# k^T v over all 128 partitions: five of nine tokens on the lower half, four on the upper, two heads at a time

## The chip, the cores and the metric

The kernel runs on one core of a Trainium2 chip. The metric is the device time of one execution in microseconds (us). Every kernel was run several times, and beside each experiment the kernel before ran on the same chip. A run more than 1.5% above the fastest of its kernel is called slow. TensorE is PE in the profile (PEld is its weight loading), VectorE is DVE, ScalarE ACT, GpSimd POOL, SyncE SP.

## The reference, cut to what matters

```python
batch, n_heads, seq, head_dim = (8, 8, 576, 64)          # q, k, v in float32
kv  = einsum('bhsd,bhse->bhde', k, v)                    # k^T v, 64 x 64 per head
out = einsum('bhsd,bhde->bhse', q, kv)
out = out / rms(out) * g_norm
x   = out.transpose(0, 2, 1, 3).reshape(4608, 512)
# then a mixture of 8 experts: x + gate * expert(x) where x @ w_skip > 0, else x
```

Attention reads q, k and v of eight batches, 1152 KB each. k^T v sums over the 576 tokens of a head.

Of the kernel before, what the change touches and what calls it, by code (L numbers as in the profile page):

```python
# [8 lines left out]
FP32 = mybir.dt.float32  # L9
# [8 lines left out]
def kernel(  # L18
# [9 lines left out]
    moe_w2: bass.AP,  # L28
    out: bass.AP,
):  # L30



# [29 lines left out]
    nc = tc.nc  # L63
    B, H, S, D = q.shape
    DM = H * D
    N = B * S
    P = 128
    C = S // 64
    CT = 4
# [25 lines left out]
    kv_pool = attn.enter_context(tc.tile_pool(name="kv", bufs=3))  # L95
    q_pool = attn.enter_context(tc.tile_pool(name="q", bufs=3))
    setup = attn.enter_context(tc.tile_pool(name="setup", bufs=1))
# [3 lines left out]
    xb_pool = attn.enter_context(tc.tile_pool(name="xb", bufs=2))  # L101
    ps_kv = attn.enter_context(tc.tile_pool(name="ps_kv", bufs=1, space=bass.MemoryType.PSUM))
# [7 lines left out]
    kts, vts, qts = {}, {}, {}  # L110

    def load(pool, tag, src, b):
        t = pool.tile([P, 4, C, D], FP32, tag=tag, name=tag)
        nc.sync.dma_start(out=t[:, :, :, :].rearrange("p j c d -> p j (c d)"),
                          in_=src[b].rearrange("(j a) (p c) d -> (a p) j (c d)", a=2, c=C))
        return t

    def load_first(b):

        for name, pool, src, to in (("k", kv_pool, k, kts), ("v", kv_pool, v, vts)):  # L120
            to[b] = pool.tile([P, 4, C, D], FP32, tag=name, name=name)
        for js in (slice(0, 2), slice(2, 4)):
            for src, t in ((k, kts[b]), (v, vts[b])):
                nc.sync.dma_start(
                    out=t[:, js, :, :].rearrange("p j c d -> p j (c d)"),
                    in_=src[b].rearrange("(j a) (p c) d -> (a p) j (c d)", a=2, c=C)[:, js, :])

    def load_kv(b):
        if b < B:
            kts[b] = load(kv_pool, "k", k, b)  # L130
            vts[b] = load(kv_pool, "v", v, b)

    def load_q(b):
        if b < B:
            qts[b] = load(q_pool, "q", q, b)
# [3 lines left out]



    load_first(0)
    load_q(0)

    room = xb_pool.tile([P, NQ, 2, DM], FP32, tag="xb", name="xb")
# [57 lines left out]
    for a in range(2):  # L203
        r = slice(a * 64, (a + 1) * 64)
# [4 lines left out]
    for w in range(2):  # L209
        nc.vector.tensor_copy(out=swap[:, w * 64:(w + 1) * 64],  # L210
                              in_=ident[:, (1 - w) * 64:(2 - w) * 64])
# [52 lines left out]
    for lo, m in kinds:  # L264

        t = keep.tile([P, P], FP32, name=f"again{lo}_{m}")
# [38 lines left out]


    kvns, kvTs, kvss = {}, {}, {}

    sum_ps = ps_kv.tile([P, 2, 512], FP32, name="sum_ps")[:, :, 0:2 * D].rearrange("p a (u d) -> p a u d", u=2)
    sw_ps = g_ps[:, 0:2 * PK]  # L310
    kvT_ps = g_ps[:, 0:2 * P].rearrange("p (u x) -> p u x", u=2)
    lg_ps = g_ps[:, 2 * PK:2 * PK + 8 * G].rearrange("p (u a w g) -> p u a w g", u=2, a=2, w=2)
# [4 lines left out]
        assert ap[-1] == [1, PK]  # L317
        return bass.AP(x.tensor, x.offset, ap[:-1] + [[PK - G, 2], [1, G]])

    def state(b, third):  # L320

        kt, vt = kts[b], vts[b]
        for i in range(6 * third, 6 * third + 6):
            u, c = divmod(i, C)
            for w in range(2):
                for a in range(2):
                    r = slice(a * 64, (a + 1) * 64)
                    nc.tensor.matmul(  # L328
                        out=sum_ps[w * 64:(w + 1) * 64, a, u, :],
                        lhsT=kt[r, 2 * u + w, c, :], rhs=vt[r, 2 * u + w, c, :],  # L330
                        start=(c == 0), stop=(c == C - 1), skip_group_check=True)
        if third < 2:
            return
        kvn = kvn_pool.tile([P, 2, PK], FP32, tag="kvn", name="kvn")
        nc.scalar.copy(out=kvn[:, :, G:G + 2 * D].rearrange("p u (a d) -> p a u d", a=2), in_=sum_ps)
        kvns[b] = kvn
# [44 lines left out]
    def turn(n):  # L381
        _, b, i, u = units[n]
        if i is None:
            qTs[n] = q8s[b][:, u, :, :, :]
            return
        ps = ps_q.tile([P, 2, 2, 2, 64], FP32, tag="q", name="q_ps")
        for w in range(2):
            for hf in range(2):
                c = 4 * i + 2 * hf
                nc.tensor.transpose(out=ps[:, w, :, hf, :], in_=qts[b][:, 2 * u + w, c:c + 2, :],  # L390
                                    identity=ident[:, :])
        qT = att_pool.tile([P, 2, 2, P], FP32, tag="qT", name="qT")
        nc.scalar.copy(out=qT[:, :, :, :].rearrange("p w a t -> p (w a t)"),
                       in_=ps[:, :, :, :, :].rearrange("p w a h t -> p (w a h t)"))
        qTs[n] = qT
# [282 lines left out]
    def slot_rows(cols, pool, tag):  # L678

        n = cols.stop - cols.start  # L680
        rows = pool.tile([P, n], I32, tag=f"rows{tag}", name="rows")
        nc.vector.tensor_single_scalar(out=rows[:, :], in_=srow[:, cols], scalar=float(N),
                                       op=ALU.add)
        src = pool.tile([P, n], I32, tag=f"src{tag}", name="src")
        nc.vector.scalar_tensor_tensor(out=src[:, :], in0=rows[:, :], scalar=N, in1=rows[:, :],
                                       op0=ALU.is_lt, op1=ALU.mult)
        return rows, src
# [7 lines left out]
    def early():  # L695
# [10 lines left out]
        def put():  # L706
# [14 lines left out]
            in_offset=bass.IndirectOffsetOnAxis(ap=src[:, 0:1], axis=0))  # L721

    load_kv(1)
    load_kv(2)
    load_q(1)


    zero = setup.tile([64, DM], FP32)
    nc.gpsimd.memset(zero[:, :], 0.0)
    for b in range(KNOWN // S // 4 * 4, KNOWN // S):  # L730
        nc.gpsimd.dma_start(
            out=out[b * S:(b + 1) * S, :].rearrange("(p c) d -> p c d", c=C)[:, C - 1, :],
            in_=zero[:, :])

    todo = {}

    def at(step, part, job):
        todo.setdefault((step, part), []).append(job)
# [6 lines left out]
    for n, (_, b, i, _) in enumerate(units):  # L745
        if i is not None:
            starts.setdefault(b, n)
    parts = [lambda b: state(b, 0), lambda b: state(b, 1), lambda b: state(b, 2), state_t, state_m, state_s]
    for part in parts[:5]:
        part(0)  # L750
    turn(0)
    for part in parts[5:]:
        part(0)
    for b, n in starts.items():
        if b:
            for i, part in enumerate(parts):
                at(max(n - 6 + i, (0, 0, 1, 1, 2, 3)[i]), "pe", lambda b=b, part=part: part(b))
        def loads(b=b):
            load_kv(b + 3)
            load_q(b + 2)  # L760
        at(n, "end", loads)
# [47 lines left out]
    with tc.tile_pool(name="wpool_b", bufs=1, reuse_waits="tile") as wpool_b, \  # L809
# [456 lines left out]
        rows, src = slot_rows(slice(0, NCOL), slot_pool, "")  # L1266
# [28 lines left out]
        with tc.For_i(1, n_rounds, 1):  # L1295
# [8 lines left out]
                out=left[:, :].rearrange("p (r c) -> p r c", c=CK),  # L1304
# [3 lines left out]
            rows, src = slot_rows(slice(0, NCOL), slot_pool, "")  # L1308
# [35 lines left out]
```

## The kernel before: what the change touches

A load of k puts the heads with j of 0 to 3 in the tile, a = 0 on partitions 0 to 63 and a = 1 on partitions 64 to 127. A partition holds nine consecutive tokens of one head: 9 x 64 x 4 = 2304 bytes in one packet. One DMA fills all 128 partitions.

```python
def load(pool, tag, src, b):
    t = pool.tile([P, 4, C, D], FP32, tag=tag, name=tag)          # P = 128, C = 9, D = 64
    nc.sync.dma_start(out=t[:, :, :, :].rearrange("p j c d -> p j (c d)"),
                      in_=src[b].rearrange("(j a) (p c) d -> (a p) j (c d)", a=2, c=C))
    return t
```

The products of one batch are issued in three parts. By the slices of the program, four 64x64 products go together: two halves of the input partitions (a) by two halves of the output partitions (w).

```python
def state(b, third):
    kt, vt = kts[b], vts[b]
    for i in range(6 * third, 6 * third + 6):
        u, c = divmod(i, C)
        for w in range(2):
            for a in range(2):
                r = slice(a * 64, (a + 1) * 64)
                nc.tensor.matmul(out=sum_ps[w * 64:(w + 1) * 64, a, u, :],
                                 lhsT=kt[r, 2 * u + w, c, :], rhs=vt[r, 2 * u + w, c, :],
                                 start=(c == 0), stop=(c == C - 1), skip_group_check=True)
    ...
```

Output rows are stored in two halves, partitions 0 to 63 from GpSimd's queue and 64 to 127 from SyncE's. SyncE's queue is in order (in the profile before, two stores stand in it from 64.84 us for 10.22 us, and k is issued only at 75.15), so this store also stands ahead of later loads:

```python
    nc.gpsimd.dma_start(out=rows[0], in_=xb[0:64, ...])
    return lambda: nc.sync.dma_start(out=rows[1], in_=xb[64:128, ...])     # issued one step later
    ...
    def loads(b=b):                    # at the end of the first step of batch b
        load_kv(b + 3)
        load_q(b + 2)
```

## Time and profile before

| | before |
|---|---|
| time, median of 4 runs beside the changed kernel | 418.05 us (416.71 to 419.89) |
| span of the profiled run, granted PE clock | 418.8 us, 0.935 |
| products of k^T v on PE | 26.3 us busy |

Four lines of the page: the busy time of the engines, the granted PE clock in forty slices of 10.5 us (tenths of full speed), and two of the DMA queues (packets, MB, share of 16 engines).

```profile
PE 368.3 (88%) x4292; PEld 316.6 (76%) x4292; DVE 250.8 (60%) x621; ACT 139.1 (33%) x368; POOL 118.8 (28%) x185
...
PEclk9975999889966599999999999999999999999995
...
q1 hardware_dynamic: 26688, 66.59, 45.3%
...
q8 instruction: 36, 0.59, 0.6%
```

PE is the busiest engine over the whole, but up to 73 us the DMA engines are hardly ever free. q1 is SyncE's queue, with all loads in it. q8, of the kind that the page calls instruction, moves 36 packets of about 16 KB (0.59 MB).

### The profile page before, as it was taken

What the parts mean: (1) busy time and instruction counts of PE and PEld (TensorE: products, weight loads), DVE (VectorE), ACT (ScalarE), POOL (GpSimd) and SP (SyncE); (2) the same over time, 40 slices, a digit from 0 to 9 for tenths busy, and PEclk for the clock granted to TensorE, in tenths of its full rate; (3) what the DMA queues carried; (4) which work ended last, traced back from release to release, by engine and by line L of the source; (5) the groups of instructions that cost most, each with busy time, mean ns of one, the idle gap of its engine ahead of it and who ended that gap; (6) DMA issues with size and microseconds to landing.
All of it is one profiled execution on the core that took longest, in us unless ns stands there. A gap on an engine that the chain in (4) does not pass through costs nothing. (4 is left out here: it accounts for less than half of the span.)

```text
span 418.8 us, 10468 instructions
## 1 busy us (share of the span) xinstructions
PE 368.3 (88%) x4292; PEld 316.6 (76%) x4292; DVE 250.8 (60%) x621; ACT 139.1 (33%) x368; POOL 118.8 (28%) x185
## 2 busy tenths in 40 slices
PE   3879999688684599999999999999999999999970
PEld 3768888576563486958977987988988988989950
DVE  2132576638898763166565775766776866778520
ACT  1253676446553131212420440430440431423300
POOL 3012667535546614012203301121212203201010
PEclk9975999889966599999999999999999999999995
DMA  8999999894128995055351651752772663501010
GB/s 292 392 390 391 318 396 394 223 383 122 42 71 317 354 347 176 5 223 184 120 202 48 233 210 51 250 201 69 242 225 83 230 229 102 203 1 52 0 42 8
DMA packets 31339, 81.89 MB, mean 196 GB/s; under 512 B 1866, under 2 KB 1874, under 8 KB 31284
## 3 DMA queue, kind: packets, MB, share of 16 engines
q1 hardware_dynamic: 26688, 66.59, 45.3%
q0 software_dynamic: 4576, 14.54, 10.4%
q8 instruction: 36, 0.59, 0.6%
q14 instruction: 19, 0.16, 0.1%
q10 hardware_dynamic: 20, 0.02, 0.0%
HBM read 66.80 MB, written 14.61 MB: 194 GB/s over the span
## 5 line engine op out<-in xcount | busy, mean ns | idle before, releaser
L1013 PE MATMUL bank<-xt,w 128*128 128x144 f32 (+3 forms) x336 | 56.4, 291 | 0.0
L1023 ACT COPY p<-bank 128x144 f32<-128x144 f32 (+4 forms) x70 | 21.0, 300 | 105.6 <-PE bank L1013 103.9
L1013 PEld LDWEIGHTS bank<-xt,w 128*128 128x128 f32 x336 | 47.8, 190 | 1.9 <-DVE bank L1017 1.4
L1017 DVE TENSOR_TENSOR bank<-bank,p 128x144 f32<-128x144 f32 (+4 forms) x70 | 23.8, 341 | 40.2 <-PE bank L1013 38.7
L430 PE MATMUL o_ps<-kvn,qT 64*64 64x73 f32 (+1 forms) x384 | 35.6, 276 | 8.6 <-DVE xl L459 5.7
L430 PEld LDWEIGHTS o_ps<-kvn,qT 64*64 64x64 f32 (+1 forms) x384 | 30.1, 178 | 15.8 <-issue 8.2
L1155 POOL DMA_INDIRECT out_dram<-xg,rows x16 | 16.2, 1014 | 79.1 <-DVE xg L1152 78.5
L492 POOL TENSOR_TENSOR xb<-xl,g_b 128x512 f32<-128x512 f32 x32 | 38.0, 1188 | 0.0
L1013 PE MATMUL bank<-xs,s 128*128 128x144 f32 (+3 forms) x224 | 37.3, 292 | 0.0
L945 PE MATMUL bank<-w,ht 128*32 128x128 f32 (+2 forms) x448 | 36.1, 321 | 0.0
L430 PE MATMUL o_ps<-kvs,qT 64*64 64x73 f32 (+1 forms) x384 | 34.9, 277 | 0.9 <-issue 0.9
L442 DVE TENSOR_REDUCE rs<-sq 128x8 f32<-128x512 f32 x36 | 24.5, 680 | 15.0 <-ACT sq L434 14.5
L1013 PEld LDWEIGHTS bank<-xs,s 128*128 128x128 f32 x224 | 31.6, 190 | 1.0 <-ACT p L1023 0.3
L905 POOL DMA_INDIRECT xg<-out_dram,src x15 | 15.7, 1047 | 56.5 <-PE bank L1013 36.2
L328 PE MATMUL sum_ps<-v,k 64*64 64x64 f32 x1152 | 26.3, 245 | 6.1 <-issue 5.3
L945 PEld LDWEIGHTS bank<-w,ht 128*32 128x32 f32 (+2 forms) x448 | 20.6, 121 | 14.6 <-issue 11.8
L1155 POOL DMA_INDIRECT out_dram<-xg,arows x8 | 9.0, 1130 | 77.0 <-DVE xg L1152 76.7
L459 DVE TENSOR_TENSOR xl<-o_ps,rs 128x584 f32<-128x584 f32 x36 | 27.6, 767 | 4.8 <-DVE rs L456 0.5
L328 PEld LDWEIGHTS sum_ps<-v,k 64*64 64x64 f32 x1152 | 22.9, 156 | 10.0 <-issue 9.3
L430 PEld LDWEIGHTS o_ps<-kvs,qT 64*64 64x64 f32 (+1 forms) x384 | 29.4, 178 | 1.2 <-issue 1.0
L476 POOL TENSOR_TENSOR lp<-xl 128x36 f32<-128x36 f32 x36 | 9.2, 255 | 66.5 <-DVE xl L459 66.3
L434 ACT ACTIVATE sq<-o_ps 128x512 f32<-128x512 f32 x36 | 21.5, 597 | 19.4 <-PE o_ps L430 19.2
(190 smaller groups left out, 744.8 us busy)
## 6 DMA issues: line engine op xcount, KB each, us to landing
w<-in_moe_w_dram SPq DMA_DIRECT2D x16, 2048.0 KB, 10.4
q<-in_q_dram SPq DMA_DIRECT2D x8, 1152.0 KB, 14.9
k<-in_k_dram SPq DMA_DIRECT2D x7, 1152.0 KB, 12.4
v<-in_v_dram SPq DMA_DIRECT2D x7, 1152.0 KB, 15.1
out_dram<-xb SPq DMA_DIRECT2D x8, 512.0 KB, 17.0
out_dram<-xb POOLq DMA_DIRECT2D x8, 512.0 KB, 7.6
k<-in_k_dram SPq DMA_DIRECT2D x2, 576.0 KB, 5.3
v<-in_v_dram SPq DMA_DIRECT2D x2, 576.0 KB, 8.4
```

Of the source, the lines that this page charges most:

```text
L328: nc.tensor.matmul(out=sum_ps[w * 64:(w + 1) * 64, a, u, :], lhsT=kt[r, 2 * u + w, c, :], rhs=vt[r, 2 * u + w, c, :], start=(c == 0), stop ...
L430: nc.tensor.matmul(out=ps[to, r, cols], lhsT=lhsT, rhs=kv[rows, u, a * KD:(a + 1) * KD], start=True, stop=True, skip_group_check=True)
L434: nc.scalar.activation(out=sq[:, :, :, :], in_=heads(ps, G, G + 2 * D), func=ACT.Square)
L442: nc.vector.tensor_reduce(out=rs[:, :, :], in_=sq[:, :, :, :].rearrange("p r w (a d) -> p r (w a) d", a=2), axis=AX.X, op=ALU.add)
L459: nc.vector.tensor_tensor(out=xl[:, :, :, :].rearrange("p r w (a k) -> p r (w a) k", a=2), in0=ps[:, :, 0:2 * PK].rearrange("p r (h k) -> ...
L492: nc.gpsimd.tensor_tensor(out=xb[:, :, 4 * u * D:(4 * u + 4) * D].rearrange("p r (w x) -> p r w x", w=2), in0=xl[:, :, :, G:G + 2 * D], in ...
L905: nc.gpsimd.indirect_dma_start(out=x_of(xg, off, m), out_offset=None, in_=cut_rows(m)[:, :], in_offset=bass.IndirectOffsetOnAxis(ap=idx[:, ...
L945: nc.tensor.matmul(out=yps[q * m:(q + 1) * m, 0:n], lhsT=ht[:, f, off:off + m], rhs=w_sb[r][1][:, f, q * n:(q + 1) * n], start=(f == 0), s ...
L1013: nc.tensor.matmul(out=out, lhsT=lhsT(i), rhs=rhs(i), start=start and i == 0, stop=i == k - 1, skip_group_check=True)
L1017: nc.vector.tensor_tensor(out=to, in0=x, in1=y, op=ALU.add)
L1023: nc.scalar.copy(out=t, in_=x)
L1155: ins = nc.gpsimd.indirect_dma_start(out=cut_rows(m)[:, :], out_offset=bass.IndirectOffsetOnAxis(ap=rows[:, col:col + 1], axis=0), in_=x, ...
```

## The change

The intent is to sum over all 128 input partitions at once. If both halves of them hold tokens of the same head, one 128x64 product replaces two 64x64 ones, and two heads share the 128 output partitions. Nine tokens don't split evenly, so a lower partition takes five and the upper partition beside it in the sum takes four; the fifth is multiplied over 64 rows alone. This makes 40 matmuls a batch. One DMA now fills 64 partitions.

```diff
-    load(...)            # one DMA, 128 partitions x 4 heads x 2304 bytes
+    LOW = C - CT                                               # 5; CT = 4
+    def load_halves(t, src, b, hs=slice(0, H)):
+        src = src[b].rearrange("h (p c) d -> p h (c d)", c=C)
+        for half, cs, to in ((0, slice(0, LOW), slice(0, LOW)), (1, slice(LOW, C), slice(LOW - CT, LOW))):
+            nc.sync.dma_start(
+                out=t[half * 64:(half + 1) * 64, hs, to, :].rearrange("p h c d -> p h (c d)"),
+                in_=src[:, hs, cs.start * D:cs.stop * D])
 ...
-    def state(b, third):  ...
+    def state(b, part):
+        u, a = divmod(part, 2)
+        for c in range(LOW):
+            r = slice(0, P if c else 64)
+            for w in range(2):
+                h = 4 * u + 2 * w + a
+                nc.tensor.matmul(out=sum_ps[w * 64:(w + 1) * 64, a, u, :], lhsT=kt[r, h, c, :],
+                                 rhs=vt[r, h, c, :], start=(c == 0), stop=(c == LOW - 1), ...)
 ...
-                at(max(n - 6 + i, (0, 0, 1, 1, 2, 3)[i]), "pe", ...)
+                at(max(n - 7 + i, (0, 0, 1, 1, 1, 2, 3)[i]), "pe", ...)
```

Cut away: the sums move into one PSUM bank, and a tile of zeros comes from an idle buffer.

More of the change, by code (lines that the diff above doesn't have):

```diff
@@ L116, in load, with load_kv @@
         return t
-    def load_first(b):
-        for name, pool, src, to in (("k", kv_pool, k, kts), ("v", kv_pool, v, vts)):
-            to[b] = pool.tile([P, 4, C, D], FP32, tag=name, name=name)
-        for js in (slice(0, 2), slice(2, 4)):
-            for src, t in ((k, kts[b]), (v, vts[b])):
-                nc.sync.dma_start(
-                    out=t[:, js, :, :].rearrange("p j c d -> p j (c d)"),
-                    in_=src[b].rearrange("(j a) (p c) d -> (a p) j (c d)", a=2, c=C)[:, js, :])
-    def load_kv(b):
-        if b < B:
-            kts[b] = load(kv_pool, "k", k, b)
-            vts[b] = load(kv_pool, "v", v, b)
+    LOW = C - CT
[5 more added lines that the diff above has]
+                in_=src[:, hs, cs.start * D:cs.stop * D])
+    def load_kv(b, parts=1):
+        if b < B:
+            kts[b] = kv_pool.tile([P, H, LOW, D], FP32, tag="k", name="k")
+            vts[b] = kv_pool.tile([P, H, LOW, D], FP32, tag="v", name="v")
+            for i in range(parts):
+                hs = slice(i * H // parts, (i + 1) * H // parts)
+                load_halves(kts[b], k, b, hs)
+                load_halves(vts[b], v, b, hs)
     def load_q(b):
@@ L138 @@
     order.__enter__()
-    load_first(0)
+    load_kv(0, 2)
     load_q(0)
@@ L307 @@
     kvns, kvTs, kvss = {}, {}, {}
-    sum_ps = ps_kv.tile([P, 2, 512], FP32, name="sum_ps")[:, :, 0:2 * D].rearrange("p a (u d) -> p a u d", u=2)
+    sum_ps = ps_kv.tile([P, 512], FP32, name="sum_ps")[:, 0:4 * D].rearrange("p (a u d) -> p a u d", a=2, u=2)
     sw_ps = g_ps[:, 0:2 * PK]
@@ L318, in ends_of @@
         return bass.AP(x.tensor, x.offset, ap[:-1] + [[PK - G, 2], [1, G]])
-    def state(b, third):
+    def state(b, part):
         kt, vt = kts[b], vts[b]
-        for i in range(6 * third, 6 * third + 6):
-            u, c = divmod(i, C)
+        u, a = divmod(part, 2)
+        for c in range(LOW):
+            r = slice(0, P if c else 64)
             for w in range(2):
-                for a in range(2):
-                    r = slice(a * 64, (a + 1) * 64)
-                    nc.tensor.matmul(
-                        out=sum_ps[w * 64:(w + 1) * 64, a, u, :],
-                        lhsT=kt[r, 2 * u + w, c, :], rhs=vt[r, 2 * u + w, c, :],
-                        start=(c == 0), stop=(c == C - 1), skip_group_check=True)
-        if third < 2:
+                h = 4 * u + 2 * w + a
+                nc.tensor.matmul(
+                    out=sum_ps[w * 64:(w + 1) * 64, a, u, :], lhsT=kt[r, h, c, :],
+                    rhs=vt[r, h, c, :], start=(c == 0), stop=(c == LOW - 1), skip_group_check=True)
+        if part < 3:
             return
@@ L725 @@
     load_q(1)
-    zero = setup.tile([64, DM], FP32)
-    nc.gpsimd.memset(zero[:, :], 0.0)
+    zero = xb_pool.tile([P, 2, DM], FP32, tag="x8", name="x8", bufs=1)[0:64, 0, :]
+    nc.gpsimd.memset(zero, 0.0)
     for b in range(KNOWN // S // 4 * 4, KNOWN // S):
@@ L732 @@
             out=out[b * S:(b + 1) * S, :].rearrange("(p c) d -> p c d", c=C)[:, C - 1, :],
-            in_=zero[:, :])
+            in_=zero)
     todo = {}
@@ L747 @@
             starts.setdefault(b, n)
-    parts = [lambda b: state(b, 0), lambda b: state(b, 1), lambda b: state(b, 2), state_t, state_m, state_s]
-    for part in parts[:5]:
+    parts = [lambda b, i=i: state(b, i) for i in range(4)] + [state_t, state_m, state_s]
+    for part in parts[:6]:
         part(0)
     turn(0)
-    for part in parts[5:]:
+    for part in parts[6:]:
         part(0)
@@ L756 @@
             for i, part in enumerate(parts):
-                at(max(n - 6 + i, (0, 0, 1, 1, 2, 3)[i]), "pe", lambda b=b, part=part: part(b))
+                at(max(n - 7 + i, (0, 0, 1, 1, 1, 2, 3)[i]), "pe", lambda b=b, part=part: part(b))
         def loads(b=b):
```

## The prediction

The main sum comes to 127 us at the last k and v, the step behind at about 128, 24 to 25 us late, and after 1 to 2 taken off +23, so 441 us. Its 210 GB/s is the author's estimate, a little above the 193 to 201 GB/s of the upper half's stores. The 1 to 2 us had a second ground; they were an estimate for both together. A share for the smaller packets was not in the main sum, but in the second rival it raised the 85 us to 87. The first rival is that half-width loads keep more than half the rate, 300 GB/s. That weight loads of two products might not hide behind matmuls is an assumption; the 53 ns are an estimate from the 26 ns of L945.

> **What bounds the kernel now.** The page's chain of work that ended last has one link only (the final scatter), so I read the stages instead: first the page's forty slices, then the costliest groups and DMA issues, then windows of the stage that the change touches, then the DMA and PE orders in time.
>
> ```profile
> DMA  8999999894128995055351651752772663501010
> GB/s 292 392 390 391 318 396 394 223 383 122 42 71 317 354 347 176 5 223 184 120 202 48 233 210 51 250 201 69 242 225 83 230 229 102 203 1 52 0 42 8
> ...
> L328 PE MATMUL sum_ps<-v,k 64*64 64x64 f32 x1152 | 26.3, 245 | 6.1 <-issue 5.3
> ...
> L328 PEld LDWEIGHTS sum_ps<-v,k 64*64 64x64 f32 x1152 | 22.9, 156 | 10.0 <-issue 9.3
> ...
> q<-in_q_dram SPq DMA_DIRECT2D x8, 1152.0 KB, 14.9
> k<-in_k_dram SPq DMA_DIRECT2D x7, 1152.0 KB, 12.4
> v<-in_v_dram SPq DMA_DIRECT2D x7, 1152.0 KB, 15.1
> out_dram<-xb SPq DMA_DIRECT2D x8, 512.0 KB, 17.0
> ```
>
> A slice is 10.5 us. For the first seven (to 73 us) the DMA engines are never free, at about 392 GB/s but for one slice; attention itself runs to about 138 us, and the experts follow. k^T v (L328) costs PE 26.3 us busy over eight batches. The next view has busy time of PE, PEld, DVE, ACT and POOL, then clock, DMA share and GB/s, for stretches that I chose by what the queues held.
>
> ```profile
> 20.00:40.00 20.00, 17.55 (x323) 14.87 (x322) 5.56 (x10) 8.04 (x18) 4.67 (x8) 0.67 1.05 390
> 57.00:63.00 6.00, 5.80 (x103) 4.88 (x102) 4.31 (x9) 4.73 (x13) 4.38 (x8) 1.00 1.04 404
> ...
> 101.00:103.00 2.00, 2.00 (x74) 1.81 (x64) 1.87 (x5) 1.30 (x5) 0.97 (x1) 1.00 0.99 193
> 114.00:116.00 2.00, 1.31 (x37) 1.22 (x38) 1.90 (x5) 1.20 (x4) 1.39 (x2) 0.91 1.02 201
> ```
>
> This carries my prediction. From 20 to 63 us the queue holds k, v and q, each spread over all 128 partitions: 390 to 404 GB/s. From 101 to 103 us and from 114 to 116 us the only traffic is the store of output rows from partitions 64 to 127: the share is still 1.0, all engines busy, at half the rate. The queue view of 101 to 102 us shows nothing else running.
>
> ```profile
> q1 hardware_dynamic: 48, 0.20, 95.7%
> ```
>
> The store of the lower half on the other queue follows it and is somewhat better, 225 to 303 GB/s by its windows. The orders in time:
>
> ```profile
> 64.84 10.22 SPq L509 DMA_DIRECT2D out_dram<-xb  x2
> 75.15 0.57 SPq L114 DMA_DIRECT2D k<-in_k_dram  x1
> 75.78 2.24 SPq L114 DMA_DIRECT2D v<-in_v_dram  x1
> ```
>
> ```profile
> 101.20 0.64 PE L349 MATMUL g_ps<-gw_b,kvT 128*128 128x36 f32 x4
> 101.77 0.93 PE L328 MATMUL sum_ps<-v,k 64*64 64x64 f32 x48
> 102.63 0.66 PE L390 MATMUL q_ps<-ident,q 128*128 128x128 f32 x4
> ```
>
> The last batch's k and v are issued at 75 us, behind a store, and landed by about 90; PE takes them up only at 101.77. So loads have 10 to 12 us to spare at the end, and engine work (PE early; DVE at 9.3 to 9.6 of 10 us from 110 to 130) sets the end of attention. The change must be judged by both: what it takes from PE, and whether it uses up those 10 to 12 us.
>
> [...]In this trace L945, all rows and 128x32 weights, does 32 matmuls of 128 columns in 1.08 us, (1.08 - 0.27) / 31 = 26 ns each, four in 105 ns[...].
>
> **The change part by part.**
>
> *Products.* 144 matmuls per batch (9 tokens x 16) become 40 (8 heads x 5). Now: 48 take 0.93 us at full clock, (0.93 - 0.22) / 47 = 15 ns each, 61 ns for four; 144 cost about 2.5 us of PE (2.52 in the window 47 to 57). After: 20 pairs. If a pair takes the 61 ns that four take now, 1.2 us and 1.3 saved; if two 64-column weight loads can't hide, I estimate twice 53 ns a pair (from L945's 26 ns for 32 columns), 2.1 us and 0.4 saved. Over 8 batches: 3 to 10 us. If PE stayed the path for attention, that would be the gain.
>
> *Instructions.* 832 matmuls and as many weight loads go, 1664 of PE's 8584. PE stops without a known cause for 1.3 to 2.9 us now and then (24.7, 74.8, 82.2, 105.6 us); instruction packets of about 16 KB (36 of them, 0.59 MB) suggest instruction fetch. About 6 fewer fetches, perhaps 5 us, on the same condition.
>
> *Loads.* Each k or v load becomes two, over 64 partitions each, one after the other in one queue. Bytes stay: 2 x 1152 KB = 2.36 MB per batch. At 392 GB/s this takes 6.0 us; at 210 GB/s, my choice[...], it takes 11.2: 5.2 us more per batch, 42 in all.[...] Eight issues in place of four at the head add 4 x 0.5 us on the queue, hidden behind the slower data.
>
> *Order.* The products move from 6 to 7 steps ahead of a batch's first unit and from three parts to four, so they want their data one step (about 2.7 us) earlier, and PE is in order: a late k or v holds everything behind it.
>
> *PSUM and the zero tile.* The sums share one bank, the copy out stays 256 columns; zeros come from an idle buffer. Nothing on a path.
>
> *Sum at the last k, v,* all in one queue: 2 us to start, 8 x 11.2 = 90 for k and v, 6 x 3.0 = 18 for the q loads ahead, 4 x 4.2 = 17 for the four stores of 1 MB (4.2 from the dip at 45 to 51 us): 127 us. With 6.0 in place of 11.2 the same sum is 85, where the trace has about 90, so the sum is usable. The step behind that product now starts at 102.6 us; after, at about 127 + 1. That is 24 to 25 us late, and what follows (the last batches' norms, gating, weights, experts) waits on PE's order and moves along. I take 1 to 2 off for the shorter products[...]: +23, 441 us.
>
> **The rivals.**
>
> [...]For it: the lower store's 303. Against: every upper store is at 197 to 205[...]. At 300 GB/s k and v take 7.9 us, the sum is 100 us, the spare is just used up, and PE's saving shows: 408 to 420.
>
> *Loads don't have the stores' half rate*[...]. For it: the trace has no half load. Against: [...]later weights and stores over 128 partitions reach 400. Then only packets cost,[...] PE's 3 to 10 plus some fetches come through: 405 to 414.
>
> *It is worse than half.* The smaller packets add their share on top and PE[...] falls to half clock (0.50 was granted at 30 to 40 us). At 190 GB/s: 12.4 us, the sum 137, about 452, and some on top where the clock is low.
>
> **Range and chances.** I give half rate four chances in five; it is slower in any mix below about 280 GB/s. Between 250 GB/s (9.4 us, sum 112, +9) and 190 the time goes from 427 to 452, and I widen a little: 420 to 456. Slower by over 2% (above 426) 0.8; within 2% 0.1; faster 0.1.
>
> **What would show it.** Right: the slices from 10 to about 125 us with a DMA share near 1.0 but 200 to 260 GB/s; landing of k and v lengthened by more than the byte count; new PE waits on k or v at L328, first before the second and third batch; the granted clock low in more early slices; the last k^T v at about 128 us; PE busy for the products at 10 to 20 us and the experts' stage unchanged in length. q1's bytes stay at 66.59 MB with some 8200 more packets. Wrong: GB/s near 390 in these slices with k and v landing as now. Then the half rate belongs to stores, and the sign is that of PE's saving. If the rate is halved but the end moves less than 15 us, the spare of 10 to 12 us was larger than I read it.

## The result, and the profile after

| | before | after |
|---|---|---|
| median of 4 fast runs | 418.05 us | 450.6 us (448.89 to 452.33) |
| span of the profiled run, PE clock | 418.8 us, 0.935 | 447.1 us, 0.892 |
| ratio of the times | | 1.078 (95%: 1.072 to 1.083), slower |

A ratio is the mean time of one kernel's fast runs over that of the other's in the same rounds, so it isn't quite the ratio of the medians. The medians differ by 32.6 us, the two profiled runs by 28.3.

The page of the kernel after, in the same parts as before:

```profile
PE 389.2 (87%) x3780; PEld 331.1 (74%) x3780; DVE 249.8 (56%) x621; ACT 139.7 (31%) x368; POOL 118.5 (26%) x185
...
PEclk9965555997989855999999999999999999999995
DMA  8999999999993299924275065266265544711000
GB/s 196 251 204 244 205 226 283 234 321 265 284 317 102 58 341 335 374 69 166 87 232 192 22 240 165 90 236 230 61 229 201 148 156 176 236 48 49 0 25 21
...
q1 hardware_dynamic: 35168, 66.59, 53.6%
...
L333 PE MATMUL sum_ps<-v,k 128*64 128x64 f32 (+1 forms) x640 | 40.0, 278 | 15.2 <-DMA v<-in_v_dram 13.0
...
k<-in_k_dram SPq DMA_DIRECT2D x7, 640.0 KB, 17.8
v<-in_v_dram SPq DMA_DIRECT2D x7, 640.0 KB, 19.1
```

A slice is now 11.2 us. The DMA engines are busy in the first twelve slices, to 134 us, where before they had free time from 73 us on; the bytes in q1 are the same. They move 196 to 321 GB/s in these slices, not about 392. A 640 KB load takes longer to land than a load of 1152 KB did. And PE waits 13.0 us for v where it had no such wait worth naming before.

Windows of the kernel after, with the columns that the prediction explains (busy time of five engines, clock, DMA share, GB/s):

```profile
20.00:40.00 20.00, 13.59 (x130) 10.85 (x129) 2.25 (x4) 6.02 (x13) 1.39 (x2) 0.67 1.14 204
57.00:63.00 6.00, 6.00 (x56) 5.30 (x54) 2.53 (x5) 2.12 (x5) 2.59 (x6) 0.50 1.10 234
```

These are the stretches that had 390 and 404 GB/s. (The share adds up the times of packets, so it can pass 1, as the 1.14 here.) The last view is PE's order in time, with the waits for v of the second, the third and the last batch (start, length, what ran, and in brackets the idle time before it and what ended it):

```profile
28.31 0.48 PE L333 MATMUL sum_ps<-v,k 64*64 64x64 f32 x4 [4.09 <-DMA v<-in_v_dram]
30.85 2.58 PE L333 MATMUL sum_ps<-v,k 128*64 128x64 f32 x36 [2.06 <-DMA v<-in_v_dram]
...
42.77 1.12 PE L333 MATMUL sum_ps<-v,k 128*64 128x64 f32 x16 [1.46 <-DMA v<-in_v_dram]
...
130.13 0.69 PE L333 MATMUL sum_ps<-v,k 128*64 128x64 f32 x16 [1.21 <-DMA v<-in_v_dram]
130.75 0.66 PE L394 MATMUL q_ps<-ident,q 128*128 128x128 f32 x4
```

The last wait for v ends at 130.13 us. The products of that batch started at 101.77 before. From there to the end of the span both kernels take the same time: 447.1 - 130.1 = 317.0 us and 418.8 - 101.8 = 317.0 us. So the whole loss of the profiled runs is made before the last batch's k and v are in the core; what follows, experts included, is merely later.

PE's own order shows that these 28 us are not all waits. Attention has 32 steps, each known by its transposes of q. The fourth starts at 43.83 us, in the kernel before at 27.96: 16 us late, after 11.8 us of waits for v. The next seven steps take 35.9 us where they took 25.5, and in them PE waits for nothing: it is busy throughout, at a granted clock of 0.53 for 0.75 and with the longer products. So at 79.8 us PE is 26 us late, and the last v, for which it then waits 1.21 us, adds little. In this profiled run PE and the queue of loads come late to the same point together; which of them is needed for the loss the experiments have to say.

One reading of the busy times has to be corrected here. PE's matmuls went from 4292 to 3780, 512 fewer, while the program has 8 x (72 - 40) = 256 fewer. These float32 matmuls are recorded twice each. The prediction compared 144 records with 40 matmuls; it should have been 144 with 80.

### The profile page after: what moved, and what is told of

Its sections match the earlier page's. It is cut to its first block, busy times and chain, and to the rows that moved or that the text cites. A ratio compares the mean times of both kernels' runs of the same rounds, so it can differ in the third digit from the quotient of the medians.

```text
span 447.1 us, 9467 instructions
## 1 busy us (share of the span) xinstructions
PE 389.2 (87%) x3780; PEld 331.1 (74%) x3780; DVE 249.8 (56%) x621; ACT 139.7 (31%) x368; POOL 118.5 (26%) x185
## 3 DMA queue, kind: packets, MB, share of 16 engines
q1 hardware_dynamic: 35168, 66.59, 53.6%
## 5 line engine op out<-in xcount | busy, mean ns | idle before, releaser
L333 PE MATMUL sum_ps<-v,k 128*64 128x64 f32 (+1 forms) x640 | 40.0, 278 | 15.2 <-DMA v<-in_v_dram 13.0
L333 PEld LDWEIGHTS sum_ps<-v,k 128*64 128x64 f32 (+1 forms) x640 | 32.0, 177 | 24.8 <-issue 17.1
L434 PE MATMUL o_ps<-kvn,qT 64*64 64x73 f32 (+1 forms) x384 | 38.4, 288 | 5.1 <-DVE xl L463 5.1
L434 PEld LDWEIGHTS o_ps<-kvn,qT 64*64 64x64 f32 (+1 forms) x384 | 33.0, 189 | 12.8 <-issue 6.1
L434 PE MATMUL o_ps<-kvs,qT 64*64 64x73 f32 (+1 forms) x384 | 38.0, 289 | 0.0
L460 DVE RECIPROCAL rs<-rs 128x8 f32<-128x8 f32 x36 | 7.2, 200 | 50.9 <-ACT rs L453 50.5
L446 DVE TENSOR_REDUCE rs<-sq 128x8 f32<-128x512 f32 x36 | 24.5, 680 | 18.9 <-ACT sq L438 18.6
L434 PEld LDWEIGHTS o_ps<-kvs,qT 64*64 64x64 f32 (+1 forms) x384 | 32.5, 189 | 0.0
L397 ACT COPY qT<-q_ps 128x512 f32<-128x512 f32 x32 | 18.7, 586 | 40.3 <-PE q_ps L394 40.1
L949 PEld LDWEIGHTS bank<-w,ht 128*32 128x32 f32 (+2 forms) x448 | 20.6, 121 | 14.6 <-issue 11.8
```

The costliest lines, as they stand in the source:

```text
L333: nc.tensor.matmul(out=sum_ps[w * 64:(w + 1) * 64, a, u, :], lhsT=kt[r, h, c, :], rhs=vt[r, h, c, :], start=(c == 0), stop=(c == LOW - 1), ...
L397: nc.scalar.copy(out=qT[:, :, :, :].rearrange("p w a t -> p (w a t)"), in_=ps[:, :, :, :, :].rearrange("p w a h t -> p (w a h t)"))
L434: nc.tensor.matmul(out=ps[to, r, cols], lhsT=lhsT, rhs=kv[rows, u, a * KD:(a + 1) * KD], start=True, stop=True, skip_group_check=True)
L446: nc.vector.tensor_reduce(out=rs[:, :, :], in_=sq[:, :, :, :].rearrange("p r w (a d) -> p r (w a) d", a=2), axis=AX.X, op=ALU.add)
L949: nc.tensor.matmul(out=yps[q * m:(q + 1) * m, 0:n], lhsT=ht[:, f, off:off + m], rhs=w_sb[r][1][:, f, q * n:(q + 1) * n], start=(f == 0), s ...
```

## The experiments

**Theory.** A DMA on the lower or upper 64 partitions alone moves at about half the rate, as the upper half's stores did (193 to 201 GB/s for 390 to 404), so k and v take about 11 us a batch, and that carries the loss. **Rivals.** The packets of 1280 and 1024 bytes; the products themselves and the low PE clock in the stage (0.50 in slices after); a loop through SyncE's queue, in which late stores hold back the next loads.

### The halves alone, with the products of before

```diff
+    s4 = src[b].rearrange("(j a) (p c) d -> a p j (c d)", a=2, c=C)
+    for a in range(2):
+        nc.sync.dma_start(out=t[a*64:(a+1)*64, ...], in_=s4[a])
```

Each load of k and v in the kernel before becomes two, over 64 partitions; packets keep 2304 bytes, products and order are untouched.

> The kernel before with its own products and its own 2304-byte packets; only k and v are each loaded by two DMAs over 64 partitions in place of one over 128. Theory (64-partition loads run at half rate and the queue of loads becomes the bound): 440 to 450 us, near 200 GB/s while only k and v are in flight, the last k^T v at about 125 to 135 us. Rival packets (smaller packets cost it): about 418 us, since the packets are as before. Rival products (the 128x64 products are slower on PE): about 418 us.

Measured: 448.9 us (448.18 to 450.08) beside 419.11; ratio 1.071 (1.066 to 1.075). Its window from 20 to 40 us:

```profile
20.00:40.00 20.00, 10.83 (x192) 8.87 (x190) 2.25 (x4) 5.32 (x10) 1.39 (x2) 0.83 1.05 211
```

All engines of the DMA are busy, at 211 GB/s. This one part of the change makes 29.8 us of the 32.6. The products and the small packets are not needed for the loss. Nor is the low clock in the form that it had: this kernel was granted 0.83 in the window where the changed one was granted 0.67, and it lost nearly the same. PE loses the time in another way here: up to 135 us it waits 10.0 us for v (13.0 in the changed kernel) and stops for 18.6 us without a cause that the profile shows (2.2 in the changed kernel, 9.1 in the one before). That two kernels end nearly alike, whatever PE's own losses, fits a bound by the queue of loads.

### Small packets alone

```diff
+    for cs in (slice(0, 5), slice(5, C)):
+        nc.sync.dma_start(out=t[:, :, cs, :], in_=s3[:, :, cs.start*D:cs.stop*D])
```

Two DMAs a load, each over all 128 partitions, with 1280 and 1024 bytes.

> The kernel before with its own products; k and v are each loaded by two DMAs over all 128 partitions, one with 1280-byte and one with 1024-byte packets, so packet sizes and the number of DMAs are those of the change, without its halves. Theory (half rate from 64 partitions): 417 to 422 us, 370 to 390 GB/s in the early slices. Rival packets: 440 to 450 us.

Measured: 420.54 us (417.37 to 423.27), ratio 1.003 (0.995 to 1.010), the same. The window:

```profile
20.00:40.00 20.00, 17.36 (x319) 14.48 (x318) 5.56 (x10) 8.04 (x18) 4.66 (x8) 0.67 1.07 366
```

The packets cost 6% of the rate in this window (366 for 390) and 3% from 57 to 63 us (390 for 404), and that is hidden. The number of DMAs costs nothing that can be seen.

### The changed products, loaded mostly full width

```diff
-    two DMAs over 64 partitions, five and four tokens
+    nc.sync.dma_start(out=t[:, hs, 1:LOW, :],                 # tokens 0..511, four on each of 128 partitions
+                      in_=src[b][:, 0:CT * P, :]...)
+    nc.sync.dma_start(out=t[0:64, hs, 0, :], in_=src[b][:, CT * P:S, :]...)   # the last 64 tokens
```

> The changed kernel with its products (two heads at a time over all partitions, five steps), but with other tokens on the partitions: four tokens on each of 128 partitions by one DMA, and the last 64 tokens on the lower partitions by a second, small one with 256-byte packets (an eleventh of the bytes, less than an eighth of them). Theory: most of the loss goes, 418 to 428 us, with the small packets as the open point. Rival products: it stays at 440 or above, since the products are those of the change. If the products themselves save PE time on the path, it would be below 415.

Measured: fast runs 424.75, 426.27 and 428.25 us, two slow ones at 434.67 and 445.24; ratio of the fast runs 1.020 (1.013 to 1.026), unclear by the 2% rule. Eight ninths of the bytes at full width (the expectation's "eleventh" for the rest was a slip) bring back about 25 of the 32.6 us, with the changed products in place. What is left, some 7 us over the kernel before, has three candidates that this run doesn't separate: the remaining half-width ninth, its packets of 256 bytes (q1 has 43360 packets, 8192 more than after the change), and the changed products, which below turn out to take 1.0 us more a batch. Its profiled run was a slow one, so no window of it is read.

### Only v in halves

The edit of the first experiment, for v alone.

> As e1_halves, but only v in halves, k as before. By the sum of the load queue (2 us, 8 times 3.0 + 5.9, 18 for q, 17 for stores) the last v lands at about 108 us, near the point where the kernel before takes it up anyway: 420 to 427 us, less than half of the loss of e1_halves, because the first 10 us or so are spare. If the loss were in proportion to the bytes in halves (no spare): 431 to 435 us.

Measured: 444.26 us (442.58 to 445.98), ratio 1.059 (1.053 to 1.064). This missed: half of the half-width bytes lose 25 us, 84% of what all of them lose. In the queue sum of the prediction, k at full width and v at half rate take about 6.0/2 + 11.2/2 = 8.6 us a batch, 69 in place of 90, and the spare of 10 to 12 us should have covered part of the rest.

Three things in its trace bear on this. Of its windows of 2 us between 20 and 46 us the three best moved 346, 359 and 371 GB/s, less than the 381 to 394 of before in the same windows; by the order of the queue they hold full-width loads. Those of v moved 182 to 217. From 10 to 130 us the mean over its twelve windows of 10 us is 267 GB/s, where the kernel with both in halves has 264: half as many half-width bytes, and no better rate over the stage. And PE stops longer at a place where it stopped before. First the kernel before, then this one:

```profile
23.84 0.85 PE L328 MATMUL sum_ps<-v,k 64*64 64x64 f32 x41
26.65 0.34 PE L328 MATMUL sum_ps<-v,k 64*64 64x64 f32 x7 [1.96 <-issue]
```

```profile
31.73 0.85 PE L342 MATMUL sum_ps<-v,k 64*64 64x64 f32 x41
36.10 0.34 PE L342 MATMUL sum_ps<-v,k 64*64 64x64 f32 x7 [3.51 <-issue]
```

Both stop after 41 records of 48, the same place in the program, without waiting for anything that the profile shows. That a block of instructions is fetched there was inference; no trace shows what PE waits for. In the kernel before one packet of q8 starts between 24.0 and 24.5 us, and PE stops at 24.69. The first suspicion to be tested was another one: the loop through the stores in SyncE's queue.

### Is it a loop through the stores? Three runs

```diff
-    return lambda: nc.sync.dma_start(out=rows[1], in_=xb[64:128, ...])
+    nc.gpsimd.dma_start(out=rows[1], in_=xb[64:128, ...]); return None
```

With the upper half's store on GpSimd's queue, no store stands ahead of a load. It was done to the changed kernel, to the one with v in halves, and to the kernel before as a control.

> The changed kernel with the upper half of the output rows stored from GpSimd's queue, as the lower half already is, so that no store stands behind loads in SP's queue and none holds back later loads. Theory of a plain DMA bound (the engines are busy from 5 to 134 us in the change): little, 444 to 451 us. Theory of a loop (stores stuck behind slow loads keep the two row buffers occupied, GpSimd waits, later loads are issued later): 435 us or less.

> e4_half_v (only v in halves) with the stores moved as in e6. e4 lost 25 us where my sum of its load queue left it 2 to 9; its GpSimd waited 14.2 us for its own stores, and k and v of the last batch were issued at 103 us behind a store, not at 75. If this loop made the difference, 425 to 433 us here; if it is DMA time that my sum left out, 440 or more.

> Control: the kernel before with the stores moved as in e6. Its GpSimd didn't wait for stores, so both theories say 415 to 421 us; a clear gain or loss here would have to be taken off e6 and e7.

Measured: the changed kernel 452.29 us (449.33 to 454.59), ratio 1.077, no better. With v in halves two fast runs of 438.87 and 436.36 (two slow ones, 448.02 and 443.31), so 5 to 8 us below 444.26 in runs of another job. The control 415.7 us, ratio 0.993 (0.988 to 0.997). So the loop is not the changed kernel's loss, and of what v in halves costs it can be about 3 us beyond what the control gains as well. The excess of that experiment stays open: it lies in the early stage, the DMA engines are busy in eleven of its twelve windows, and why the full-width loads and the stores between half-width ones don't reach their rate was not found out. How PE spends it: up to 135 us it waits 6.1 us for v and 6.3 for q, and stops for 14.5 us without a cause that the profile shows, where the kernel before has 0.9, none and 9.1.

The changed kernel with the stores moved also has something to say of the clock. One of its four fast runs was granted 0.950 in the mean, the others 0.888 or 0.889; it took 451.35 us, they 449.33 to 454.59. A higher clock did not win the loss back.

### The two halves on two queues

```diff
-            nc.sync.dma_start(
+            (nc.scalar if half and b < 3 else nc.sync).dma_start(
```

The test: if transfers of two queues mix the halves, well above 210 GB/s; if they serialize, 200 to 225.

> The changed kernel; for the first three batches the upper halves of k and v are issued from the scalar engine's queue, the lower halves from SP as in the change. Only the rate of the first 25 us is to be read, not the time (the scalar engine may be held up by its issues). [...]the rate goes well above 210 GB/s, to 300 or more. If two half transfers serialize whatever their queues[...], it stays at 200 to 225 GB/s.

Measured in one look: 452.31 us. Both queues moved data together only at the start. The window from 3 to 8 us, and its queues:

```profile
3.00:8.00 5.00, 0.00 (x0) 0.00 (x0) 0.00 (x0) 0.00 (x0) 1.32 (x2) 1.00 1.10 234
```

```profile
q1 hardware_dynamic: 541, 0.66, 64.3%
q10 hardware_dynamic: 533, 0.51, 46.0%
```

The shares are shares of time that the packets took; 0.66 and 0.51 MB in 5 us are together 234 GB/s, no more than the 253 of the changed kernel in these 5 us. Later ScalarE held its issues back until 17.9 us, as it had other work in its order. So for as long as the two ran together there was no gain; the run doesn't show more, and I call it inconclusive on whether lower and upper loads can be made to fill each other's gaps. One window of the changed kernel says that something can: from 98 to 100 us, with q1 carrying half-width loads and GpSimd's queue a store of the lower half, 356 GB/s were moved. In the trace's records of packets 240 of q1's 349 have the 1024 bytes of the upper half's loads.

```profile
q1 hardware_dynamic: 349, 0.39, 63.5%
q0 software_dynamic: 95, 0.32, 40.1%
```

### Even and odd partitions in place of lower and upper

```diff
-    for a in range(2):
-        nc.sync.dma_start(out=t[a*64:(a+1)*64, ...], in_=s4[a])
+    for r in range(2):
+        nc.sync.dma_start(out=t[r:P:2, ...], in_=s3[r:P:2])
```

This is the first experiment again: two DMAs over 64 partitions each, 2304-byte packets, products of before, the same tile in the end. Only which partitions, and with them which rows of the source, go into the same DMA is different.

> As e1_halves (the products and packets of the kernel before, k and v loaded by two DMAs of 64 partitions each), but one DMA takes the even partitions and the other the odd ones, in place of the lower and the upper. Number of partitions, packets, bytes, DMAs and queue are those of e1. If what counts is where the partitions lie[...], the rate goes back to 350 GB/s or more and the time to 417 to 423 us. If it is the count of 64 partitions, or two DMAs in place of one[...], it stays near 200 GB/s and 445 to 452 us.

Measured: 421.62 us (418.67 to 422.37) beside 417.61; ratio 1.008 (1.002 to 1.015).

```profile
20.00:40.00 20.00, 18.60 (x409) 15.89 (x407) 7.03 (x13) 11.03 (x25) 5.57 (x12) 1.00 1.05 390
```

390 GB/s in place of 211, and 448.9 us become 421.6. The half rate comes neither from a DMA having 64 partitions nor from the number of DMAs. Here it could still be the rows of the source that go into one DMA; the next run leaves these as the changed kernel has them, DMA for DMA, and changes in its loads only the partitions, and it has 364 GB/s where the changed kernel had 204. So what counts is where the 64 partitions lie. The runs show the rates, 211 and 390; why the place counts no run shows.

### The change on even and odd partitions

```diff
-                out=t[half * 64:(half + 1) * 64, hs, to, :].rearrange("p h c d -> p h (c d)"),
+                out=t[half:P:2, hs, to, :].rearrange("p h c d -> p h (c d)"),
...
-            kts[b] = kv_pool.tile([P, H, LOW, D], FP32, tag="k", name="k")        # and v
+            kts[b], vts[b] = kbufs[b % 3], vbufs[b % 3]     # three standing tiles, slot 0 set to zero once
...
-            r = slice(0, P if c else 64)
+            r = slice(0, P)
```

Even partitions hold five tokens, odd ones four and a slot of zeros that no load touches, so all five products run over 128 rows.

> The change with five tokens on the even and four on the odd partitions, in place of lower and upper; the odd partitions' empty slot is set to zero once in each of three standing buffers, so that all five products run over all partitions. This gives the products of the change without its half rate. From the profile of the change five pairs of 128x64 products take about 0.95 us and six groups of four 64x64 products 0.93, so a batch has 4 x 0.95 in place of 3 x 0.93 us: nothing to gain, up to 1 us a batch to lose where PE is the path: 417 to 426 us. If the 1024 fewer PE instructions or the fewer products are worth what the change hoped for: 412 or less. If loads still ran at half rate: 445 or more.

Measured: fast runs 410.75, 410.85 and 411.64 us, one slow at 418.64; beside 419.3 before; ratio 0.983 (0.973 to 0.994). That is faster than both kernels: the interval lies below 1, though by the 2% rule the verdict against the kernel before is unclear. My main expectation, that nothing is gained, missed. First the window from 20 to 40 us; then, from the page, the traffic, the instruction packets and the products; then one part of 20 product records in PE's order.

```profile
20.00:40.00 20.00, 18.03 (x275) 15.05 (x274) 6.57 (x13) 10.18 (x23) 4.88 (x9) 0.91 1.08 364
```

```profile
GB/s 203 371 364 366 374 379 385 374 377 189 106 127 402 332 340 22 179 93 209 129 142 169 164 208 91 199 244 73 218 233 105 207 209 137 176 1 53 0 44 7
...
q8 instruction: 32, 0.52, 0.5%
...
L338 PE MATMUL sum_ps<-v,k 128*64 128x64 f32 x640 | 28.4, 241 | 6.2 <-DMA v<-in_v_dram 5.2
```

```profile
97.36 0.80 PE L338 MATMUL sum_ps<-v,k 128*64 128x64 f32 x20
```

Four parts of 0.80 us make 3.2 us a batch, no less than three of 0.93 us, 2.8 us, before; 28.4 us busy in all, for 26.3. The products are not cheaper even here. Where it gains is in time order. By the state's transposes it stands level with the previous experiment up to the fifth batch (67.7 us, the other 67.0); the next step takes 11.0 us, in the other 17.1 and in the kernel before 17.0. In that stretch the other two have these stops, here from the weight loads of the previous experiment and from the matmuls of the kernel before:

```profile
74.50 0.65 PEld L344 LDWEIGHTS sum_ps<-v,k 64*64 64x64 f32 x34 [2.24 <-issue]
...
82.89 0.18 PEld L446 LDWEIGHTS o_ps<-kvs,qT 64*64 64x64 f32 x1 [4.50 <-issue]
```

```profile
76.77 0.69 PE L328 MATMUL sum_ps<-v,k 64*64 64x64 f32 x31 [1.95 <-issue]
...
85.16 0.38 PE L430 MATMUL o_ps<-kvn,qT 64*64 64x73 f32 x1 [2.94 <-issue]
```

In the version here no stop of more than 0.9 us is left from 70 to 88 us. One comes later, of 1.17 us, and it has 32 packets of instructions for 36. Of the two kernels with halves, too, the one with fewer instructions has fewer stops: 2.2 us for 18.6. That the stops are fetches, and that fewer instructions took two of them out, is inference: in the kernel before one packet of q8 starts between 74.0 and 74.5 us and one between 82.5 and 83.0, by its stops from 74.82 and 82.22. Shown is only that the stops are gone from this stretch, and with them 6 us.

### The same with all stores on GpSimd's queue

> e10 with the upper half of the output rows stored from GpSimd's queue, which took 0.75% off the kernel before (e8). If that gain comes with any kernel whose loads are not halves: 2 to 4 us below e10; a version that beats the kernel before only if e10 is within 1 us of it.

Measured: 410.62 us (410.1 to 414.61), ratio 0.984 (0.975 to 0.994), again unclear by the 2% rule. The 0.7% that this edit gave the kernel before isn't added here; I don't know why.

## Why the prediction was right, and where its terms were not

The time was predicted at 441 us and slower; it is 450.6, within the range. By its own steps:

**Half rate of the loads: right, and shown by taking it apart.** 210 GB/s was chosen. Stretches with k and v alone have 193 to 209, the first experiment 211. That it was the halves is shown by the first experiment (halves alone: 448.9) against the even and odd one (421.6). Of the rivals, two fall: the loads did not keep 300 GB/s in these stretches, and they have the half rate (193 to 211 GB/s) as the upper half's stores do (193 to 201). The third, worse than half, was partly right. It had about 452 us at 190 GB/s, and the kernel came out at 450.6 with 193 to 209; of the three, its number is nearest, and the prediction's 210 was somewhat too kind.

**The sum at the last k, v: right, though PE came late by itself too.** Predicted 127 us for the data, about 128 for the step behind; PE's wait for the last v ends at 130.13 and that step starts at 130.75. That PE would be 26 us late already at 79.8 us, busy at a low clock and with only 1.21 us left to wait for this v, the prediction's main sum did not have; its third rival names a half clock. The spare of 10 to 12 us was used up as argued: the step is 28.1 us late (102.63 before) where the prediction made the queue 42 us longer.

**"I take 1 to 2 off": not found.** Nothing was won back: the 317.0 us from the last v to the end are the same. So +23 should have been left at +25, and the trace has +28.3.

**The products: wrong.** "144 matmuls per batch become 40", with 3 to 10 us of PE saved, mixed the records of the trace with the matmuls of the program. It is 72 to 40 matmuls, 144 to 80 records; 18 groups of four matmuls become 20 pairs of matmuls, so 36 groups of four records become 40 pairs of records. A part of 20 records takes 0.95 us at full clock, (0.95 - 0.22) / 19 = 38 ns a record, so a pair of records takes 77 ns where a group of four took 61. The batch costs 3.8 us of PE in place of 2.8. In the even and odd version it is (0.80 - 0.22) / 19 = 31 ns, about 61 a pair: a pair of 128-row products costs what four 64-row products do (61 ns). Why, no run isolates. So there was no gain in the products; that four 64x64 products had used all 128 input and output partitions before, too, is the author's reading of it. It cost little here: the first experiment, with the products of before, was 1.7 us faster (448.9 for 450.6, from different rounds). The 40.0 us busy are partly products at half clock.

**The instructions: half right.** For the same reason 1024 went, not 1664, and 4 packets of instructions, not 6. "Perhaps 5 us" for fetches, an estimate, could not show behind the half-rate loads. Once they were gone, the version on even and odd partitions came out 8 us below the kernel before, where the sum of PE's work gives nothing; the stops are the likely place.

**Packets and order: right.** The cost of the packets was put within the uncertainty of the rate; 6% and 3% were measured in two windows, hidden. The DMA engines were busy up to 134 us, so the issues in SyncE's queue were no bound.

**What was to show it.** The low GB/s at a full DMA share, the longer landing, the waits for v before the second and third batch, the low clock in early slices, and 8480 more packets at the same 66.59 MB all came. The low clock (0.50 from about 27 to 78 us) did stretch PE's steps (seven of them took 35.9 us at 0.53, where they had taken 25.5 at 0.75, with the longer products in them), but it doesn't set the time by the runs: with the stores moved, 451.35 us at 0.950 stands beside 449.33 to 454.59 at 0.888 and 0.889, and the first experiment had more clock in the window from 20 to 40 us and nearly the same time. Why it was low no run isolates.

**A window read wrongly.** The prediction took the 404 GB/s from 57 to 63 us for loads over all 128 partitions. GpSimd's queue moved 0.52 MB of a lower-half store in it. So the trace of before already held half-width traffic that ran beside other traffic without loss, which is on the side of the prediction's first rival, that half-width traffic keeps more than half the rate; with k and v one after the other in one queue the half rate came all the same.

**What stays open.** The half-and-half experiment: v alone in halves should by the prediction's sum have lost about 8 x (8.6 - 6.0) = 21 us less the spare, so some 10, and lost 25. The store loop explains about 3. The sum of durations in one queue came out for the changed kernel (127 for 130 us), and not for the one in which k and v alternate between full and half width.

## What to carry to other kernels

Before a layout is changed for PE, count what it does to a DMA: not how many partitions one transfer has, but whether these are spread over the whole range. In these runs a lower or upper half loaded at half rate (204 to 211 GB/s), the even or odd partitions at full rate or nearly so (364 to 390). And a test with the suspected part alone, here a two-line edit of the loads, settles in one run what a profile of the whole change can only suggest.
